# Sampled value rows fetched by SyncE at register addresses, two batches per transfer, with SyncE's queue in written order

## The chip, the core and the metric

The kernel runs on one core of one Trainium2 chip. A core has five engines with instruction queues of their own: TensorE (PE, with its weight loads shown as PEld), VectorE (DVE), ScalarE (ACT), GpSimd (POOL) and SyncE (SP), which here only issues DMAs. Sixteen DMA engines serve the core. The metric is the device time of one execution in microseconds (us), the median of the runs shown.

## What is computed

Block-sparse attention over 4 batches, 8 heads, 768 positions, head size 64, and then a mixture of experts with limited capacity on its output.

```python
block, n_blocks, window = 32, 24, 1
scores = scale * np.matmul(q, k.transpose(0, 1, 3, 2))
mask = np.abs(blk_i - blk_j) <= window
mask = mask | (blk_i == 0) | (blk_j == 0) | (blk_i == n_blocks - 1) | (blk_j == n_blocks - 1)
for qb in range(n_blocks):
    for kb in sampled_blocks[qb]:          # three per query block, the same for every batch and head
        mask[qb * block:(qb + 1) * block, kb * block:(kb + 1) * block] = True
...
attn = np.exp(scores); attn = attn / (np.sum(attn, axis=-1, keepdims=True) + 1e-09)
x = np.matmul(attn, v)                     # rows of all heads side by side: (3072, 512)
...
for e in range(8):                         # each row goes to its best expert, 80 rows at most for each
    h = np.maximum(x[tok_idx] @ w1[e], 0.0)
    out[tok_idx] = gate_w[tok_idx, None] * (h @ w2[e])
```

A query block sees at most eight key blocks: its window of three, the first and the last block, and the three that `sampled_blocks` names. Which blocks these are is known only when the kernel runs.

## The kernel before

The attention works in 24 groups. A group is one batch b and four neighbouring query blocks j (three at either end of the sequence); `ORDER` lists the pairs (j, b), batches 0 and 1 in its first half and 2 and 3 in its second, and `SWAP` exchanges the second and the third group of a half, so that groups 0 and 1 are both of batch 0. A group has two halves of four heads. A half goes through `products` (L352: scores of every block against its eight key blocks), `stage_a` (L360 on DVE: mask and minimum; L364 on ACT: exponent), `stage_b` (L372: transposes on PE; L338 or L340: copies out of PSUM, one on ACT and one on DVE) and `stage_c` (L386: the product with the values). On PE all of this stands in an order written by hand, in steps (`run_step`, `at`): four steps for a half, `products` at its step 0, `stage_b` at step 2, `stage_c` at step 5, which is one step after the `products` of the next half. The other engines' queues, SP's among them, are ordered by the compiler's scheduler.

Keys: `load_k` brings a batch's keys to the tile kt, and copies by DVE, ACT and POOL (`gather_k`, L291, L295, L245, L249) lay the key blocks of each group into one of two tiles kx. The sampled ones are read from kt at an address in a register; `load_blocks` (12 block numbers) and `load_own` (22 block numbers on each of DVE, ACT and POOL) put the numbers into registers (L261) at the very start. The first and the last block are copied by `fill_k_global` (L258, eight copies) whenever the batch of a kx tile changes.

Values: a group has for each of its query blocks a tile vw (the window's three blocks, 96 rows, and one global block) and a tile vd (three sampled blocks, 96 rows, and the other global block), in four sets (`SLOTS`). SP brings the windows (`load_qv`, L315) and, when the batch of a set changes, the global blocks (`load_v_global`, L238 to L242). The sampled rows are gathered by POOL: `gather_v` (L319), one indirect DMA for each query block and batch, 88 in all, with a table of row numbers, `idxV`, that DVE and POOL compute at the start (L172 to L181). For groups 1 to 5 (`VLATE`) these DMAs are put behind a key copy on POOL.

```python
nc.gpsimd.indirect_dma_start(
    out=vd[s][k][0:96, :], out_offset=None, in_=v[:, :],
    in_offset=bass.IndirectOffsetOnAxis(ap=idxV[0:96, b, qb:qb + 1], axis=0))
```

SP also loads the queries (L310, three tiles in turn), stores each group's rows to DRAM (`route1`, L409), writes zeros to the output (L754, behind the last query load) and loads rows for the blocks that see everything (`load_full`, L325 and L329). After the attention the experts run, from a store of the rows in DRAM and weights that SP loads (L869).

Of the kernel before, what the change touches and what calls it, by code (L numbers as in the profile page):

```python
# [24 lines left out]
P = 128  # L25
# [3 lines left out]
VW = HP * PW  # L29
# [6 lines left out]
VLATE = (1, 2, 3, 4, 5)  # L36
# [23 lines left out]
SWAP = (0, 1)  # L60
ORDER = []
for half in range(2):
    ORDER += [(j, 2 * half + i) for j in JO for i in range(2)]
# [5 lines left out]
SLOTS = [(0, 2, 1, 3, 0, 1, 2, 3, 0, 1, 2, 3)[n % NH] for n in range(len(ORDER))]  # L69
# [16 lines left out]
def kernel(  # L86
# [34 lines left out]
    nc.vector.tensor_copy(sf, si.rearrange("p (n t) -> p n t", t=2)[:, :, 0])  # L121
# [24 lines left out]
    with ExitStack() as actx:  # L146
# [23 lines left out]
        r32 = apool.tile([P, 1], F32, name="r32")  # L170
        for s in range(4):
            nc.gpsimd.iota(r32[32 * s:32 * s + 32, :], pattern=[[0, 1]], base=0, channel_multiplier=1,  # L172
                           allow_small_or_imprecise_dtypes=True)
        idxf = apool.tile([P, B, NBLK], F32, name="idxf")
        idxV = apool.tile([P, B, NBLK], U32, name="idxV")
        for s in range(NRAND):
            nc.vector.tensor_scalar(idxf[32 * s:32 * s + 32, 0, :], sbF[32 * s:32 * s + 32, :, s],
                                    float(BLK), r32[32 * s:32 * s + 32, :], op0=ALU.mult, op1=ALU.add)
        for b in range(1, B):
            nc.vector.tensor_scalar(idxf[0:96, b, :], idxf[0:96, 0, :], float(b * S), None, op0=ALU.add)  # L180
        nc.vector.tensor_copy(idxV[0:96], idxf[0:96])  # L181

# [34 lines left out]
        vw, vd = [[[(vp if s < 2 else apool).tile([P, VW], F32, name=f"{n}{s}{k}") for k in range(4)] for s in range(4)]  # L217
# [10 lines left out]
        def load_k(b):  # L228
            t = ktp.tile([P, HP, S], F32, name=f"kt{b % 2}", bufs=1)
            for c in ((slice(0, 2), slice(2, 4)) if b == 0 else (slice(0, 4),)):  # L230
                nc.sync.dma_start(t[:, c], kT[b][:, c])
            KT[b] = t

        def load_v_global(b, s):
            first, last = v[b * S:b * S + BLK, :], v[b * S + (NBLK - 1) * BLK:(b + 1) * S, :]
            for k in range(4):
                if k % 2 == 0:
                    nc.sync.dma_start(vw[s][k][0:32, :], last)  # L238
                    nc.sync.dma_start(vd[s][k][96:128, :], first)
                else:  # L240
                    nc.sync.dma_start(vw[s][k][96:128, :], first)
                    nc.sync.dma_start(vd[s][k][96:128, :], last)  # L242
# [61 lines left out]
        last_load = [None]  # L304

        def load_qv(b, j, s):

            t = qts[nq[0] % NQ]
            nq[0] += 1
            ld = nc.sync.dma_start(t, qn[b, j].rearrange("h d a c k -> (h d) a c k"))  # L310
            QT[b, j] = t
            last_load[0] = ld.ins
            for k, qb in enumerate(qbs_of(j)):
                lo = 32 if k % 2 == 0 else 0
                nc.sync.dma_start(vw[s][k][lo:lo + 96, :], v[b * S + (qb - 1) * BLK:b * S + (qb + 2) * BLK, :])  # L315

        def gather_v(b, j, s):
# [413 lines left out]
        if ORDER[1][1] == 1:  # L731
            load_k(1)
# [348 lines left out]
```

## Time and profile before

| | |
|---|---|
| median of 3 runs | 506.76 us (506.35 to 511.46) |
| the profiled execution | 510.95 us, its span 509.2 us |
| granted TensorE clock, mean over the span | 0.92 |
| PE busy | 407.6 us (80%) |
| DVE busy | 353.3 us (69%) |
| ACT busy | 310.4 us (61%) |
| POOL busy | 223.5 us (44%) |
| DMA | 109.34 MB, mean 215 GB/s |

A page of the profile and a packed trace of one execution are there. "Busy" is the time in which an engine worked on something; the time between is idle, and a view of the trace names what ended it: another engine's instruction, a DMA's landing, or "issue", when the engine waited for nothing that the profile shows. PEclk is the clock that TensorE was granted, as a share of 2.4 GHz; it is either 1.0 or 0.5 (1.2 GHz) at any time, and values between are means over a stretch. The DMA share is the mean busy share of the sixteen DMA engines; overlapping packets can take it a little over 1. Instructions that load registers are not counted as busy.

### The profile page before, as it was taken

Reading aid. Unit: us, or ns where it says so; the run is one execution under the profiler, and the core shown is the slowest. Engines: PE = TensorE matmul, PEld = TensorE weight load, DVE = VectorE, ACT = ScalarE, POOL = GpSimd, SP = SyncE. Lnnn points to the kernel's source line nnn. Section 1 sums busy time; section 2 is a strip of 40 time slices with the busy share of each in tenths; the row PEclk is TensorE's granted clock in tenths of the full one; section 3 lists DMA queues with packets and bytes.
Section 4 is the critical chain, followed back from the end, with each engine's and each line's share of the span. In section 5 each row is a group of like instructions: output and inputs, shape, how many; then the busy total and the mean of one; then the engine's idle time right before and its main releaser. Section 6 shows DMA issues by size and latency. Waiting matters only on the chain. (4 is left out here: it accounts for less than half of the span.)

```text
span 509.2 us, 16785 instructions
## 1 busy us (share of the span) xinstructions
PE 407.6 (80%) x6285; PEld 269.7 (53%) x6286; DVE 353.3 (69%) x1413; ACT 310.4 (61%) x748; POOL 223.5 (44%) x457
## 2 busy tenths in 40 slices
PE   0478877988898887778788899888758799898983
PEld 0245444665566554555556566665544565565651
DVE  3444665575668576887778879876986799787760
ACT  3244555565657776666656675788784475668740
POOL 3544854423542344554552435217436445242271
PEclk9888897898999988998999999997868899899997
DMA  8966889967664988896774877398406886889801
GB/s 250 285 178 191 226 257 261 260 191 239 172 177 145 302 239 223 216 270 201 224 217 116 253 210 202 111 311 289 125 23 192 283 273 209 291 295 310 324 17 30
DMA packets 57658, 109.34 MB, mean 215 GB/s; under 512 B 7196, under 2 KB 19485, under 8 KB 57187
## 3 DMA queue, kind: packets, MB, share of 16 engines
q1 hardware_dynamic: 50914, 88.17, 56.0%
q0 software_dynamic: 6656, 20.02, 14.8%
q8 instruction: 52, 0.85, 0.7%
q14 instruction: 36, 0.29, 0.2%
HBM read 94.38 MB, written 13.99 MB: 213 GB/s over the span
## 5 line engine op out<-in xcount | busy, mean ns | idle before, releaser
L319 POOL DMA_INDIRECT vd<-in_v_dram,idxV x88 | 84.6, 962 | 91.3 <-PE xb L386 71.4
L364 ACT ACTIVATE sb<-sb,mn 128x256 f32<-128x256 f32 (+1 forms) x192 | 86.5, 501 | 46.7 <-DVE mn L360 43.8
L360 DVE CUSTOM_DVE_ANT_1 sb<-S,quad 128x256 f32<-128x256 f32 (+1 forms) x192 | 74.9, 417 | 40.8 <-PE S L352 20.8
L372 PE MATMUL pt<-ident,sb 128*128 128x128 f32 (+1 forms) x384 | 72.5, 303 | 31.2 <-ACT sb L364 22.6
L352 PE MATMUL S<-kx,qt 64*32 64x256 f32 x1408 | 68.5, 437 | 15.4 <-DVE quad L207 11.7
L879 DVE TENSOR_TENSOR whl<-raw,whl 128x1024 fp32r<-128x1024 f32 x53 | 71.3, 1376 | 12.3 <-ACT whl L878 12.2
L878 ACT CAST whl<-raw 128x1024 fp32r<-128x1024 f32 x64 | 63.8, 1044 | 21.1 <-DMA raw<-in_w_dram 17.6
L372 PEld LDWEIGHTS pt<-ident,sb 128*128 128x128 f32 (+1 forms) x384 | 44.0, 152 | 53.6 <-ACT sb L364 33.9
L386 PE MATMUL xb<-vd,pts 128*32 128x65 f32 x1408 | 60.1, 230 | 10.2 <-issue 10.0
L386 PE MATMUL xb<-vw,pts 128*32 128x65 f32 x1408 | 59.0, 234 | 7.8 <-issue 6.8
L386 PEld LDWEIGHTS xb<-vd,pts 128*32 128x32 f32 x1408 | 42.9, 116 | 14.8 <-issue 14.8
L352 PEld LDWEIGHTS S<-kx,qt 64*32 64x32 f32 x1408 | 32.2, 142 | 34.3 <-issue 29.0
L386 PEld LDWEIGHTS xb<-vw,pts 128*32 128x32 f32 x1408 | 39.6, 115 | 18.2 <-issue 13.1
L879 POOL TENSOR_TENSOR whl<-raw,whl 128x1024 fp32r<-128x1024 f32 x11 | 29.7, 2707 | 42.3 <-ACT whl L878 42.3
L340 DVE COPY pts<-pt 128x512 f32<-128x512 f32 (+1 forms) x48 | 30.9, 643 | 23.0 <-PE pt L372 21.1
L926 PE MATMUL ph<-whl,xh 128*80 128x512 f32 x128 | 42.2, 401 | 0.9 <-ACT xh L886 0.6
L959 PE MATMUL po<-whl,hh 128*80 128x512 f32 x112 | 37.2, 403 | 2.4 <-DVE ob L965 2.0
L295 ACT COPY kx<-kt 128x128 f32 (+1 forms) x96 | 24.0, 296 | 20.4 <-PE S L352 12.3
L245 POOL COPY kx<-kt 128x128 f32 x84 | 22.4, 305 | 26.6 <-PE S L352 15.2
L525 DVE TENSOR_SCALAR_CACHE_REDUCE dump<-keyrow,keycol,cnt 128x640 bf16<-128x640 f32 (+5 forms) x36 | 32.4, 900 | 0.1
L585 ACT COPY xs<-xb 128x260 f32<-128x260 f32 (+2 forms) x64 | 23.3, 365 | 6.8 <-PE xb L386 6.0
L338 ACT COPY pts<-pt 128x512 f32<-128x512 f32 (+1 forms) x48 | 26.3, 548 | 1.5 <-PE pt L372 0.8
(210 smaller groups left out, 769.1 us busy)
## 6 DMA issues: line engine op xcount, KB each, us to landing
raw<-in_w_dram SPq DMA_DIRECT2D x64, 512.0 KB
vw<-in_v_dram SPq DMA_DIRECT2D x88, 195.0 KB
x_dram<-xs SPq DMA_DIRECT2D x24, 260.0 KB
vf<-in_v_dram SPq DMA_DIRECT2D x24, 260.0 KB
qt<-in_qn_dram SPq DMA_DIRECT2D x24, 256.0 KB
out_dram<-zero SPq DMA_DIRECT2D x12, 512.0 KB
kt<-in_kT_dram SPq DMA_DIRECT2D x3, 1536.0 KB
vw<-in_v_dram SPq DMA_DIRECT2D x32, 65.0 KB
```

What stands on the lines that cost most here:

```text
L319: nc.gpsimd.indirect_dma_start(out=vd[s][k][0:96, :], out_offset=None, in_=v[:, :], in_offset=bass.IndirectOffsetOnAxis(ap=idxV[0:96, b, q ...
L340: nc.vector.tensor_copy(dst, src)
L352: nc.tensor.matmul(banks[h][BLK * k:BLK * k + BLK, i].rearrange("p (g a) c -> p g (a c)", g=2), lhsT=QT[b, j][d, hp, :, k], rhs=keys, star ...
L360: ins = nc.vector.tensor_tensor_reduce(out=sb, in0=st, in1=quad[0:r, j, :, None].to_broadcast([r, 8, 32]), scale=-0.125, scalar=3.0e38, op ...
L364: order["s"] = nc.scalar.activation(p, p, AF.Exp, bias=mn, scale=-1.0).ins
L372: nc.tensor.transpose(pt[:, (2 * i + c) * r:(2 * i + c + 1) * r], p[:, c * P:(c + 1) * P], ident[0:r, 0:r])
L386: nc.tensor.matmul(xb[place:place + 32, o:o + 65], lhsT=pts[:, c * r + BLK * k:c * r + BLK * k + BLK], rhs=(vw, vd)[c][s][k][:, hd * 65:hd ...
L525: cmp = nc.vector.tensor_scalar(d, keyrow[:, lo * P:hi * P], key, c, op0=ALU.is_le, op1=ALU.add, accum_out=c)
L878: nc.scalar.copy(hi, t)
L879: eng.tensor_sub(lo, t, hi.bitcast(F32))
L926: nc.tensor.matmul(ps[0:SLOT, :], lhsT=l[:, cs], rhs=r[:, ws], start=(i == 0), stop=(i == 3 * HP - 1))
L959: nc.tensor.matmul(po[0:SLOT, :], lhsT=l[:, cs], rhs=r[:, ws], start=(i == 0), stop=(i == 23))
```

## The change

- The indirect DMAs of POOL and the table `idxV` are gone. The sampled rows come by SP's DMAs, one for each query block and sampled block, whose source row stands in a register of SP. `load_rows` loads the 12 (or 9) block numbers of a pair of groups into SP's registers.
- A transfer covers two batches: groups 2p and 2p+1 are the same query blocks j in two batches (`SWAP` is gone), and vw and vd are now two sets, one for each pair in turn, with room for four query blocks and two batches. A window's DMA brings 192 rows, a sampled block's 64. For the first pair alone the batches are loaded apart.
- SP's DMAs of the attention stand in the order in which they are written. At step 2 of each even group come the values of the next pair; the store of zeros has a step of its own.
- `load_own` (22 register loads on each of three engines) moves behind the first scores (DVE) and exponents (ACT).
- With `SWAP` gone, a kx tile changes its batch less often: of the nine calls of `fill_k_global` for a whole tile (groups 1 to 4 and 12 to 16), the six for groups 2, 3, 4, 14, 15 and 16 fall away: 48 copies, 36 of them on DVE.
- The copy of the numbers to `sf` moves from DVE to ACT, and a POOL drain late in the attention is dropped.

```diff
-VLATE = (1, 2, 3, 4, 5)
-    if half in SWAP:
-        ORDER[12 * half + 1], ORDER[12 * half + 2] = ORDER[12 * half + 2], ORDER[12 * half + 1]
+ORDER = [(j, 2 * half + i) for half in range(2) for j in JO for i in range(2)]
...
-    nc.vector.tensor_copy(sf, si.rearrange("p (n t) -> p n t", t=2)[:, :, 0])
+    nc.scalar.copy(sf, si.rearrange("p (n t) -> p n t", t=2)[:, :, 0])
...
-        idxV = apool.tile([P, B, NBLK], U32, name="idxV")
...
-        vw, vd = [[[(vp if s < 2 else apool).tile([P, VW], F32, name=f"{n}{s}{k}") for k in range(4)] for s in range(4)]
+        vw, vd = [[(vp if i < 1 else apool).tile([P, 4, 2, VW], F32, name=f"{n}{i}") for i in range(2)]
...
+        def load_v_global(i, b):
+            first, last = vrows[0:BLK, b], vrows[(NBLK - 1) * BLK:, b]
+            for dst, lo, k0, src in ((vw[i], 0, 0, last), (vw[i], 96, 1, first), (vd[i], 96, 0, first),
+                                     (vd[i], 96, 1, last)):
+                nc.sync.dma_start(dst[lo:lo + 32, k0:4:2, b % 2], src[:, None].to_broadcast([BLK, 2, VW]))
...
-            for r, e in enumerate((ENG.DVE, ENG.Activation, ENG.Pool)):
-                vals = read_blocks(slice(NRAND + r, (NBLK - 1) * NRAND, NRAND), [e])
+            for r, (e, last) in enumerate(((ENG.DVE, "v"), (ENG.Activation, "s"), (ENG.Pool, None))):
+                with tc.issue_after(order[last]) if last else nullcontext():
+                    vals = read_blocks(slice(NRAND + r, (NBLK - 1) * NRAND, NRAND), [e])
...
+        def load_rows(pair):
+            if 2 * pair < len(ORDER):
+                qbs = qbs_of(ORDER[2 * pair][0])
+                c = min(qbs) * NRAND
+                vals = read_blocks(slice(c, c + len(qbs) * NRAND), [ENG.SP])
+                for k, qb in enumerate(qbs):
+                    for r in range(NRAND):
+                        ROWS[pair, k, r] = vals[(qb - min(qbs)) * NRAND + r] * BLK
...
+        def load_v(pair, bs=None):
...
+            def window(k):
+                lo, row = 32 if k % 2 == 0 else 0, (qbs[k] - 1) * BLK
+                nc.sync.dma_start(vw[i][lo:lo + 96, k, at_b], vrows[row:row + 96, bs])
+            def sampled(k, r):
+                nc.sync.dma_start(vd[i][32 * r:32 * r + 32, k, at_b], vrows[bass.ds(ROWS[pair, k, r], BLK), bs])
...
-        with tc.manual_schedule(engines={ENG.PE}):
+        with tc.manual_schedule(engines={ENG.PE, ENG.SP}):
+            run(load_k(0))
+            load_q(0)
+            load_v_global(0, 0)
+            load_rows(0)
+            fs, ks = load_v(0, slice(0, 1)), load_k(1)
+            run(fs[:10] + ks[:1] + fs[10:] + ks[1:])
+            load_q(1)
+            nc.sync.dma_start(wg, w_gate.rearrange("(c p) e -> p c e", p=P))
+            load_v_global(0, 1)
+            run(load_v(0, slice(1, 2)))
+            load_rows(1)
             for n, (j, b) in enumerate(ORDER):
+                if n == 0:
+                    prefetch(0)
+                    at(1, load_own)
                 at(0, lambda n=n: prefetch(n + 1))
-                at(2 if (n + 2) % NH in (1, 5) else 0, lambda n=n: loads(n + 2))
+                at(0, lambda n=n: load_q(n + 2))
...
+                if n and n % 2 == 0 and n + 2 < len(ORDER):
+                    def next_v(pair=n // 2 + 1):
+                        if pair in (6, 7):
+                            for b in range(2, 4):
+                                load_v_global(pair % 2, b)
+                        run(load_v(pair))
+                        load_rows(pair + 1)
+                    at(2, next_v)
```

## Rows read from the trace of the kernel before

**Rows 1.** The busy time of each engine in stretches of the span: before the first score product, from there to the first `products` of group 5, from there to the first of group 12, and from there to the end of the last `stage_c`. After each engine's busy time the number of its instructions; the last three columns are the mean granted clock, the DMA share and the DMA rate.

```profile
0.00:14.96 14.96, 0.70 (x2) 0.53 (x3) 6.68 (x46) 5.52 (x25) 6.06 (x28) 1.00 0.84 257
14.96:105.78 90.82, 71.04 (x1194) 43.67 (x1194) 49.49 (x270) 42.85 (x117) 46.53 (x93) 0.87 0.86 237
105.78:200.33 94.55, 79.76 (x1527) 54.35 (x1524) 62.41 (x312) 63.92 (x173) 40.00 (x107) 0.94 0.73 211
200.33:367.90 167.57, 141.22 (x2971) 96.39 (x2967) 131.81 (x621) 113.20 (x304) 74.26 (x190) 0.95 0.72 211
```

**Rows 2.** The timeline from the start to the first copies out of PSUM: DVE, ACT and the first score products of PE. Columns: start, duration, engine, line, operation, in brackets the idle time before.

```profile
3.75 0.15 DVE L168 COPY capv<-misc 128x1 f32<-128x1 f32 x1
8.79 0.75 DVE L177 TENSOR_SCALAR idxf<-sbF,r 32x24 f32<-32x24 f32 x3 [4.89 <-POOL tri L141]
...
9.57 0.23 DVE L189 TENSOR_TENSOR dif<-sbF,qbI 128x72 f32<-128x72 f32 x1
...
14.21 0.18 DVE L207 COPY quad<-m 32x32 f32<-32x32 f32 x1
14.42 3.23 DVE L249 COPY kx<-kt 128x64 f32<-128x64 f32 x20
22.42 0.42 DVE L360 CUSTOM_DVE_ANT_1 sb<-S,quad 128x256 f32<-128x256 f32 x1 [4.77 <-remote]
...
22.89 1.71 ACT L364 ACTIVATE sb<-sb,mn 128x256 f32<-128x256 f32 x4 [9.22 <-DVE mn L360]
24.67 0.59 ACT L338 COPY pts<-pt 128x512 f32<-128x512 f32 x1
...
14.96 3.37 PE L352 MATMUL S<-kx,qt 64*32 64x256 f32 x32 [11.74 <-DVE quad L207]
```

**Rows 3.** The register loads of L261, by engine: duration in ns (least, median, most), and the first and the last start in us. Each engine's shorter one loads 12 numbers, its longer one 22.

```profile
L261 ACTq TENSOR_LOAD <-sbi x2: 986/2814/4643, 2.4 to 3.4; - x2
L261 DVEq TENSOR_LOAD <-sbi x2: 1120/3041/4962, 2.4 to 3.7; - x2
```

**Rows 4.** All engines between 2 and 8 us, columns as in the first group: the loads of the first keys and queries.

```profile
2.00:8.00 6.00, 0.70 (x2) 0.50 (x2) 0.59 (x4) 0.00 (x0) 1.00 (x7) 1.00 0.98 341
```

**Rows 5.** The timeline of POOL's indirect DMAs (before the first score of DVE, and around the `stage_c` that begins at 33.00) and of PE in that `stage_c`.

```profile
17.85 0.92 POOL L319 DMA_INDIRECT vd<-in_v_dram,idxV  x1 [0.30 <-issue]
...
33.34 0.92 POOL L319 DMA_INDIRECT vd<-in_v_dram,idxV  x1 [0.30 <-issue]
...
34.91 0.29 PE L386 MATMUL xb<-vw,pts 128*32 128x65 f32 x3 [0.43 <-issue]
36.38 0.22 PE L386 MATMUL xb<-vw,pts 128*32 128x65 f32 x1 [1.18 <-issue]
```

**Rows 6.** PE's matmuls and weight loads of L386 alone, in the windows that hold one `stage_c` each, for the fifteen near which POOL issued indirect DMAs: the first and the sum of the five up to 90 us, and the first and the sum of the ten after that. The second column is the window's length, then PE and PEld busy, clock, DMA share and rate.

```profile
33.00:38.42 5.42, 2.37 (x64) 1.55 (x64) 1.00 0.57 150
...
sum 15.42, PE 9.31 PEld 6.46; mean PE 1.86 PEld 1.29
...
120.85:126.02 5.17, 3.06 (x64) 1.95 (x64) 0.81 0.93 273
...
sum 32.20, PE 20.40 PEld 13.89; mean PE 2.04 PEld 1.39
```

**Rows 7.** The same for ten others, with no indirect DMA near: one in full DMA traffic, and the sum of the ten.

```profile
189.08:190.22 1.14, 1.11 (x48) 0.95 (x48) 1.00 0.97 296
...
sum 11.41, PE 11.20 PEld 9.56; mean PE 1.12 PEld 0.96
```

**Rows 8.** PE on either side of a quiet `stage_c`: its last matmuls, and the first transposes of the half that comes next.

```profile
226.74 0.30 PE L386 MATMUL xb<-vd,pts 128*32 128x65 f32 x8
228.40 0.33 PE L372 MATMUL pt<-ident,sb 128*128 128x128 f32 x1 [1.36 <-ACT sb L364]
```

**Rows 9.** All engines in the stretches at half clock that begin during or right after the `stage_c` and score product named in the groups above: the first and the sum of the four up to 94 us, and the sum of the four between 124 and 234 us.

```profile
21.61:28.43 6.82, 4.89 (x84) 3.30 (x88) 2.93 (x14) 2.60 (x6) 0.00 (x0) 0.50 1.05 317
...
sum 17.07, PE 14.76 PEld 8.74 DVE 5.58 ACT 6.83 POOL 3.65; mean PE 3.69 PEld 2.18 DVE 1.40 ACT 1.71 POOL 0.91
...
sum 13.64, PE 13.35 PEld 8.86 DVE 5.93 ACT 7.24 POOL 4.46; mean PE 3.34 PEld 2.22 DVE 1.48 ACT 1.81 POOL 1.12
```

**Rows 10.** Groups of instructions by line: copies of the global key blocks (one group for each engine) and POOL's indirect DMAs; count, busy us, mean ns, idle before.

```profile
L258 DVE COPY kx<-kt 128x128 f32<-128x128 f32 x54 | 9.1, 228 | 6.3 <-PE misc L491 3.9 <-PE cs L540 2.1 <-PE S L352 0.3
L258 ACT COPY kx<-kt 128x128 f32<-128x128 f32 (+1 forms) x26 | 6.2, 282 | 7.0 <-PE cs L540 3.5 <-PE misc L491 3.5
L319 POOL DMA_INDIRECT vd<-in_v_dram,idxV x88 | 84.6, 962 | 91.3 <-PE xb L386 71.4 <-issue 13.5 <-DVE tmp L193 2.3
```

**Rows 11.** SP's timeline (the time from one issue to the next lies in the start column): a global block of 32 rows, four windows of 96 rows, and the last issue before and the first after a long pause. The last two rows are of the DMA view: the size of a window's transfer, and the packets, MB and share of POOL's queue.

```profile
10.65 0.31 SPq L241 DMA_DIRECT2D vw<-in_v_dram  x1
...
12.25 1.84 SPq L315 DMA_DIRECT2D vw<-in_v_dram  x4
...
21.84 0.34 SPq L310 DMA_DIRECT2D qt<-in_qn_dram  x1
38.84 0.33 SPq L409 DMA_DIRECT2D x_dram<-xs  x1
...
vw<-in_v_dram SPq DMA_DIRECT2D x88, 195.0 KB
...
q0 software_dynamic: 6656, 20.02, 14.8%
```

More of the change, by code (lines that the diff above doesn't have):

```diff
@@ L302, in gather_k, with load_q @@
             return todo
-        last_load = [None]
-        def load_qv(b, j, s):
+        def load_q(n):
+            if n >= len(ORDER):
+                return
+            j, b = ORDER[n]
             t = qts[nq[0] % NQ]
             nq[0] += 1
-            ld = nc.sync.dma_start(t, qn[b, j].rearrange("h d a c k -> (h d) a c k"))
+            nc.sync.dma_start(t, qn[b, j].rearrange("h d a c k -> (h d) a c k"))
             QT[b, j] = t
[L312 to L317, printed above, removed]
-            for k, qb in enumerate(qbs_of(j)):
-                nc.gpsimd.indirect_dma_start(
-                    out=vd[s][k][0:96, :], out_offset=None, in_=v[:, :],
-                    in_offset=bass.IndirectOffsetOnAxis(ap=idxV[0:96, b, qb:qb + 1], axis=0))
+        ROWS = {}
+        def load_rows(pair):
[7 more added lines that the diff above has]
+        def load_v(pair, bs=None):
+            j, b = ORDER[2 * pair]
+            i, qbs = pair % 2, qbs_of(j)
+            bs = bs or slice(b, b + 2)
+            at_b = slice(bs.start % 2, bs.start % 2 + bs.stop - bs.start)
+            def window(k):
[3 more added lines that the diff above has]
+                nc.sync.dma_start(vd[i][32 * r:32 * r + 32, k, at_b], vrows[bass.ds(ROWS[pair, k, r], BLK), bs])
+            return ([lambda k=k: window(k) for k in range(len(qbs))]
+                    + [lambda k=k, r=r: sampled(k, r) for k in range(len(qbs)) for r in range(NRAND)])
         def load_full(b):
@@ L376, in stage_b, with stage_c @@
             return [pts[:, 2 * i * r:2 * (i + 1) * r] for i in range(len(ps))]
-        def stage_c(xb, j, s, items):
+        def stage_c(xb, j, s, xb_b, items):
             r = rows_of(j)
@@ L578, in f @@
                     def f():
-                        stage_c(xb, j, s, [(store[i], 4 * half + i) for i in ids])
+                        stage_c(xb, j, n // 2 % 2, b % 2, [(store[i], 4 * half + i) for i in ids])
                     return f
@@ L679, in fresh @@
             return n < bufs or ORDER[n - bufs][1] != ORDER[n][1]
-        def fresh_v(n):
-            before = [m for m in range(n) if SLOTS[m] == SLOTS[n]]
-            return not before or ORDER[before[-1]][1] != ORDER[n][1]
         def prefetch(n):
@@ L711, in prefetch @@
                     at(GLATE + i * (8 - GLATE) // len(todo), g)
-                    if n in VLATE and i == len(todo) - 1:
-                        def h():
-                            with tc.issue_after(order["p"]):
-                                gather_v(b, j, SLOTS[n])
-                        at(7, h)
                 else:
                     at(i * 6 // len(todo), f)
-        def loads(n):
-            if n < len(ORDER):
-                j, b = ORDER[n]
-                load_qv(b, j, SLOTS[n])
-                if n not in VLATE:
-                    gather_v(b, j, SLOTS[n])
-                if fresh_v(n):
-                    load_v_global(b, SLOTS[n])
@@ L739, with second @@
             for n, (j, b) in enumerate(ORDER):
                 m = n % NH
+                if n == 0:
+                    prefetch(0)
+                    at(1, load_own)
                 at(0, lambda n=n: prefetch(n + 1))
-                at(2 if (n + 2) % NH in (1, 5) else 0, lambda n=n: loads(n + 2))
+                at(0, lambda n=n: load_q(n + 2))
+                if n == 0:
+                    def second():
+                        for b in range(2):
+                            load_v_global(1, b)
+                        run(load_v(1))
+                        load_rows(2)
+                    at(0, second)
```

63 lines of the change are left out of this document (14 added, 49 removed).

## The prediction

> **What bounds the kernel now.** I read the stretches of the span first [rows 1]. The last `stage_c` ends at 367.9 us; the experts take the remaining 141 us, and the change does not touch their work, so everything is decided before. From the first score on PE is busy 78 to 84% of each stretch, DVE 54 to 79%, the DMA engines 72 to 86%; POOL is busy half of the time or less. So PE's own queue sets the pace. Until 14.96 us PE has almost nothing to do. Then I asked what PE loses inside its work, by looking at one kind of work that is the same 48 times, `stage_c`. Ten of them take 1.14 us each, as the sum 11.41 shows [rows 7]. Fifteen others take 47.62 us together, 3.2 us each, for the same matmuls [rows 6]. In the long ones PE stands still for 0.4 to 1.2 us at a time in front of instructions with no wait ("issue"), and all fifteen lie beside POOL's indirect DMAs, which follow each other every 1.2 us [rows 5]. Traffic as such is not it: a quiet one ran with the DMA engines 97% busy, a long one with 57% [rows 6, 7]. The same shows at the first scores: the products end on PE at 18.33, yet DVE gets them at 22.42, and in between POOL issues gathers [rows 2, 5]. PE's clock follows: eight stretches at half clock begin in or just behind such places [rows 9].
>
> **Gathers leave POOL.** 88 instructions of 0.96 us go [rows 10]; POOL is idle half of the time, so its 84.6 us count as 0 (up to 1 if a key copy was late). What counts is PE. Excess of the long `stage_c`: 47.62 - 15 x 1.14 = 30.5 us. The window from 120.85 had a mean clock of 0.81, some 1 us of half clock; I leave 29.4. Not all comes back. After a quiet `stage_c` PE waited 1.36 us for ACT before its next transposes [rows 8], a wait that a long one swallows; the ten later long ones average 3.22 us, 2.08 over 1.14, so 0.72 of 2.08 would be left, 35%. That is the low end, 10.3 us; the high end is all, 29.4. In the first stretches DVE is far from full (54%), later it is at 79%, so I take 60%: 17.6 us. The Trainium skill ("SBUF — State Buffer", Who interferes with whom) says the opposite: PE and ACT never wait on anyone. The 1.14 against 3.2 us disagrees in time, though not yet in cause; by the page this term would be 0.
>
> **Half clock.** In the eight stretches PE was busy 14.76 + 13.35 = 28.1 us [rows 9]; at full clock half of it, 14 us, is saved. Other idle time can still lower the clock, and DVE paces some of these halves: I take 7, between 0 and 14.
>
> **Register loads behind the first scores.** Now DVE is done with `capv` at 3.90, loads 22 numbers for 4.96 us [rows 2, 3], starts on the mask at 8.79 with three instructions for the table, and runs from 9.57 to 14.39 to `quad`; 20 key copies end at 17.65, the products 0.7 us later. After the change the same chain of 4.8 us starts at 3.9: mask 8.7, copies 12.0, products 12.7. The keys (2 x 768 KB) and queries (256 KB) are there: 2.05 MB had come by 8.0 us [rows 4]. With the 4.1 us of waiting gone as well, DVE's first score comes at 12.8, 9.6 us sooner. But the loads now stand between the exponents and the copies out of PSUM: exponents end 2.2 us after the first score, at 15.0, ACT's 4.64 us [rows 3] make it 19.6, where the first copy stood at 24.67 [rows 2]. Behind them wait these copies, and behind those PE's `stage_c`. Gain 5; it is 9.6 if the loads find cover, and 1 if the scores still wait 4.1 us.
>
> **The key copies.** 48 of 80 global copies go: 36 x 0.228 us on DVE, 12 x 0.28 on ACT, 11.6 us [rows 10], most of it beside PE's work. In the last stretch DVE is nearly as full as PE: I take 2, between 0 and 5.
>
> **SP.** It gains 144 DMAs for sampled rows and twelve register loads, and loses 40 window DMAs and half of the 64 global ones. A 32-row DMA takes SP 0.31 us, a 96-row one 0.46 [rows 11]; one with 64 rows and a register is not in the trace. Bounds: 0.31, and the 1.22 us from one gather to the next on POOL [rows 5]; I take 0.45, since the queue and the kind of issue are those of the first. A pair then costs 12 x 0.45 + 4 x 0.7 + 1.1 for the register loads, about 9 us (at 1.22: 19 us), against the 29 us that a pair lasts now (353 us for twelve [rows 1]): 0 on the path. Queued behind SP's waits are the loads of the pair after, and for those PE's `stage_c`. The written order also ends pauses such as the one from 22.2 to 38.84, where SP stood before a store of rows with the loads of two groups behind it [rows 11]. But the loads themselves set a floor. Up to 105.78 us the DMA engines were busy 0.84 x 14.96 + 0.86 x 90.82 = 90.7 us [rows 1]: no more than 15 us can be won there, and my terms put 5 + 0.6 x 9.7 + 0.5 x 7.4 = 14.5 us there. Rates that close to 100% don't last, and the second batch's keys are now needed one group sooner: -3, between 0 and -8.
>
> **Sum.** 5 + 17.6 + 7 + 2 - 3 = 28.6 us. The profiled execution took 510.95 us, 1.4 of it outside its span, so its like would take 482.4. It is 4.2 us above the median; I take the saving off the median: 506.76 - 28.6 = 478.2. Low ends together give 1 + 10.3 + 0 + 0 - 8 = 3.3 us (503), high ends 9.6 + 29.4 + 14 + 5 = 58 us (449).
>
> **Rivals.**
> 1. *DMA becomes the bound.* The stalls go, but two sets of values instead of four leave little slack: a pair's loads may start only when the pair before the last is done with its set. For it: DMA shares of 0.86 before 105.78 and 0.72 later at 10% less time leave bursts near 1. Against: those bursts exist now, and nothing on PE waited for values. It keeps some 10 to 18 us of the 28.6: 489 to 497.
> 2. *The stalls stay,* since they come with the gathered rows' arrival and not with POOL's issuing; the rows now arrive by SP. For: in the traffic of the long ones the gathers' packets are always there too. Against: windows of 195 KB with rows of the same length come all the time, and quiet `stage_c` run under 97%. Left are 1 us of the start and 2 of copies: 503. The page named above, which lets PE wait on nobody, would lead to this result.
> 3. *Slower: the sampled rows are slow in SP's queue.* One mechanism: 64 rows a DMA, each behind SP's waits, at a rate well below that of the gathers (20 MB in 14.8% of the span [rows 11], 266 GB/s). A pair moves 1.6 MB of sampled rows and about 4.3 MB of the rest; at the 296 GB/s of a full stretch [rows 7] the rest takes 15 us. If the sampled rows come below 100 GB/s, a pair needs 31 us instead of 29 and PE waits in every pair: 506.8 + 11 x 2 - 5 for the start = 524. At POOL's 1.22 us each, 133 KB would come at 109 GB/s, just above that point.
> 4. *Nothing changes*, because the scheduler's new order on DVE and ACT costs what PE wins: 507.
>
> **How the numbers follow.** Forecast (462 to 489) 0.60; DMA bound (489 to 500) 0.18; stalls stay (503) 0.08; slower 0.10; nothing 0.04. A measurement of this kernel can tell about 1%, 5 us, from no change. Faster: 0.60 + 0.18 and 0.02 of the third, 0.80; same 0.10; slower 0.10. The range leaves out the slower and the unchanged case and the far low end: 458 to 503.
>
> **What would show it.** All `stage_c` at 1.1 to 1.3 us; DVE's first score within 0.3 us of the end of the products, near 13 us; a gap of 5 us on DVE and ACT right after it; PE's clock in 14.96 to 105.78 above 0.87, and fewer half-clock stretches; the last `stage_c` near 340; POOL busy some 85 us less; the experts' part still near 141 us. I am wrong if long `stage_c` remain with no gathers on POOL (2), if PE waits on landings of vw or vd (1, 3), or if the first copy out of PSUM comes later than 21 us.

## The result, and the profile after

On the chip of the first measurement the changed kernel took 492.25 us (median of 4 runs, 488.19 to 497.25) and the kernel before 507.64 (506.35 to 511.46): ratio 0.966, 95% interval 0.957 to 0.975. The forecast was 478. The profiled execution took 488.19 us with a span of 486.4.

That ratio does not hold on every chip. All runs of one comparison share a chip, and later comparisons fell on others (the number of the first chip is not on record; it may be chip 0 too). Some runs came 1.5 to 3% above the fastest of their kernel and are left out of the ratios; without them the median of the kernel before on chip 10 is 472.4 us, and that of the kernel with key copies made again (below) 499.65.

| chip | kernel before, us | changed kernel, us | ratio, 95% interval |
|---|---|---|---|
| first measurement | 507.64 | 492.25 | 0.966 (0.957 to 0.975) |
| 0 | 509.31 | 491.18 | 0.965 (0.956 to 0.973) |
| 10 | 473.62 | 491.39 | 1.039 (1.033 to 1.046) |
| 4 | 475.43 | only variants of it, 489 to 502, and one at 548 | |
| 2 | 474.98 | only variants of it, 494 and 500 | |

The changed kernel takes the same time in all three comparisons, 491 to 492 us; it is the kernel before that has two times. So the result is faster by 3.5% twice and slower by 3.9% once, where all seven runs of the kernel before (471 to 485 us) lie below all four of the changed one (489 to 495), and the explanation has to hold both. Chips where the kernel before takes 507 to 509 us are called the first kind below, those where it takes 474 to 475 us the second. Each numbered chip was used in one comparison only, so whether the kind goes with the chip or with the hour is not told apart.

First the stretches of the changed kernel (columns as in [rows 1]): up to the first score product, to the first `products` of group 5, to the first of group 12, to the end of the last `stage_c`.

```profile
0.00:8.98 8.98, 0.70 (x2) 0.52 (x3) 5.62 (x38) 4.74 (x21) 2.09 (x20) 1.00 0.75 250
8.98:98.79 89.81, 68.48 (x1193) 46.00 (x1193) 45.63 (x246) 45.27 (x125) 13.10 (x60) 0.89 0.92 232
98.79:180.55 81.76, 71.84 (x1527) 49.98 (x1524) 60.96 (x306) 60.41 (x162) 19.11 (x82) 0.98 0.72 191
180.55:345.64 165.09, 139.84 (x2971) 96.19 (x2967) 129.49 (x606) 111.50 (x298) 43.47 (x162) 0.94 0.81 222
```

The first products begin 6.0 us sooner, DVE's first score 11.0 (11.46 against 22.42 us [rows 2]), group 5 begins 7.0 us sooner, group 12 19.8, and the last `stage_c` ends 22.3 us sooner. The second stretch is as long as before (89.81 against 90.82 us): what the start won was not added to there, although the stalls of [rows 6] are gone: 27 of the 48 `stage_c` take 1.11 or 1.12 us. What PE does in it instead shows in the waits, up to the end of the last `stage_c` (us in total, times, longest; the 5.9 us are the start, before the first product), and in group 2's first `stage_c`: its window (length, PE and PEld busy, clock, DMA share, rate) and PE's timeline.

```profile
PE xb L382 <- DMA vd<-in_v_dram: 9.1, 9, 1.9
PE S L348 <- DVE kx L225: 5.9, 1, 5.9
PE xb L382 <- DMA vw<-in_v_dram: 5.1, 3, 2.4
PE xb L382 <- issue: 2.1, 2, 1.3
```

```profile
45.09:58.21 13.12, 4.24 (x64) 2.62 (x64) 0.63 1.05 241
```

```profile
46.73 0.30 PE L382 MATMUL xb<-vw,pts 128*32 128x65 f32 x2 [1.33 <-DMA vw<-in_v_dram]
48.34 0.30 PE L382 MATMUL xb<-vw,pts 128*32 128x65 f32 x2 [1.31 <-DMA vw<-in_v_dram]
51.08 0.42 PE L382 MATMUL xb<-vw,pts 128*32 128x65 f32 x2 [2.44 <-DMA vw<-in_v_dram]
...
55.64 0.40 PE L382 MATMUL xb<-vd,pts 128*32 128x65 f32 x2 [1.17 <-DMA vd<-in_v_dram]
```

A `stage_c` that takes 1.1 us when its values are there runs from 45.09 to 58.20 us, matmul after matmul released by the landing of the next rows. In SP's timeline the same stretch looks like this (start, duration of the merged group):

```profile
25.38 7.94 SPq L314 DMA_DIRECT2D vd<-in_v_dram  x12
34.18 0.36 SPq L287 DMA_DIRECT2D qt<-in_qn_dram  x1
...
39.34 1.90 SPq L311 DMA_DIRECT2D vw<-in_v_dram  x4
41.44 11.96 SPq L314 DMA_DIRECT2D vd<-in_v_dram  x12
```

Twelve sampled DMAs of 32 rows take SP 7.94 us, 0.66 us each, and the first twelve of 64 rows 11.96 us, 1.0 us each; the forecast had 0.45 for the latter.

### The profile page after: what moved, and what is told of

The parts are those of the page before. It is cut to its first block, busy times and chain, and to the rows that moved or that the text cites. A ratio compares the mean times of both kernels' runs of the same rounds, so it can differ in the third digit from the quotient of the medians.

```text
span 486.4 us, 16932 instructions
## 1 busy us (share of the span) xinstructions
PE 395.4 (81%) x6286; PEld 267.9 (55%) x6286; DVE 344.4 (71%) x1369; ACT 308.3 (63%) x737; POOL 141.4 (29%) x365
## 5 line engine op out<-in xcount | busy, mean ns | idle before, releaser
L368 PE MATMUL pt<-ident,sb 128*128 128x128 f32 (+1 forms) x384 | 67.4, 294 | 21.6 <-ACT sb L360 20.6
L348 PE MATMUL S<-kx,qt 64*32 64x256 f32 x1408 | 67.0, 434 | 10.6 <-DVE kx L225 5.9
L877 DVE TENSOR_TENSOR whl<-raw,whl 128x1024 fp32r<-128x1024 f32 x53 | 67.0, 1294 | 8.7 <-ACT whl L876 8.3
L368 PEld LDWEIGHTS pt<-ident,sb 128*128 128x128 f32 (+1 forms) x384 | 42.6, 148 | 40.5 <-ACT sb L360 35.5
L382 PE MATMUL xb<-vd,pts 128*32 128x65 f32 x1408 | 57.2, 236 | 9.4 <-DMA vd<-in_v_dram 7.2
L382 PE MATMUL xb<-vw,pts 128*32 128x65 f32 x1408 | 56.8, 240 | 7.8 <-DMA vw<-in_v_dram 5.1
L469 POOL TENSOR_SCALAR tab<-oh_all 128x8 bf16<-128x8 f32 x23 | 5.3, 232 | 167.2 <-DVE oh_all L453 167.1
L382 PEld LDWEIGHTS xb<-vd,pts 128*32 128x32 f32 x1408 | 41.9, 121 | 11.7 <-issue 9.9
L924 PE MATMUL ph<-whl,xh 128*80 128x512 f32 x128 | 43.8, 415 | 0.6 <-ACT xh L884 0.6
L877 POOL TENSOR_TENSOR whl<-raw,whl 128x1024 fp32r<-128x1024 f32 x11 | 30.0, 2727 | 48.6 <-ACT whl L876 48.5
L957 PE MATMUL po<-whl,hh 128*80 128x512 f32 x112 | 36.2, 393 | 1.9 <-DVE ob L963 1.9
```

The source lines that it names most:

```text
L348: nc.tensor.matmul(banks[h][BLK * k:BLK * k + BLK, i].rearrange("p (g a) c -> p g (a c)", g=2), lhsT=QT[b, j][d, hp, :, k], rhs=keys, star ...
L368: nc.tensor.transpose(pt[:, (2 * i + c) * r:(2 * i + c + 1) * r], p[:, c * P:(c + 1) * P], ident[0:r, 0:r])
L382: nc.tensor.matmul(xb[place:place + 32, o:o + 65], lhsT=pts[:, c * r + BLK * k:c * r + BLK * k + BLK], rhs=(vw, vd)[c][s][:, k, xb_b, hd * ...
L877: eng.tensor_sub(lo, t, hi.bitcast(F32))
L924: nc.tensor.matmul(ps[0:SLOT, :], lhsT=l[:, cs], rhs=r[:, ws], start=(i == 0), stop=(i == 3 * HP - 1))
L957: nc.tensor.matmul(po[0:SLOT, :], lhsT=l[:, cs], rhs=r[:, ws], start=(i == 0), stop=(i == 23))
```

## The experiments

**Gathers on POOL again.** The twelve sampled DMAs of a pair became eight gathers (POOL's indirect DMAs); the table of indices came back with them, the POOL drain that the change had dropped did not.

```
...
-   nc.sync.dma_start(vd[i][32 * r:32 * r + 32, k, at_b], vrows[bass.ds(ROWS[pair, k, r], BLK), bs])
+   nc.gpsimd.indirect_dma_start(
+       out=vd[i][0:96, k, c % 2, :], out_offset=None, in_=v[:, :],
+       in_offset=bass.IndirectOffsetOnAxis(ap=idxV[0:96, c, qbs[k]:qbs[k] + 1], axis=0))
...
```

> The changed kernel with its sampled rows fetched by 88 indirect DMAs on POOL again (0.96 us each, one per query block and batch, 96 rows), into the same two-batch tiles and at the same steps; SP has no register loads and no sampled DMAs. The rest of the change stays. Theory (POOL's issuing stops PE): PE's idle pieces of over 0.35 us in front of instructions that wait for nothing, 3 us in sum in the attention part of the changed kernel against 15 in the kernel before, come back to 10 to 15 us, many stage_c are at 2 to 3.2 us instead of 1.12, and the time is 500 to 508 us. Rival (they came with the old order of loads or of key copies, not with POOL): stage_c stay at 1.12 us and the time is within 3 us of 492.

On chip 4, 501.76 us beside 475.43 of the kernel before. The time is in the range of the theory, its mechanism is not there, and 9 us of the time lie behind the last matmul (see the end of the next section). The windows of six `stage_c` with gathers within 2 us of them:

```profile
67.80:68.97 1.17, 1.17 (x64) 1.00 (x64) 1.00 1.09 292
...
sum 6.97, PE 6.95 PEld 6.00; mean PE 1.16 PEld 1.00
```

1.16 us each, with POOL's gathers beside them, against 3.2 in [rows 6]. These six are not all: 35 `stage_c` lie within 2 us of a gather, and 21 of them take at most 1.21 us, the longest 4.9. In front of their matmuls PE stands 8.9 us without a wait, in 7 pieces; the changed kernel, without gathers, has 8.1 us in 6 on chip 10. The kernel before at 475 us was the first sign that this chip differs from the first.

**Gathers of nearly no bytes.** In the changed kernel, 88 gathers of 32 bytes a row go to a tile that nobody reads.

```
...
+   nc.gpsimd.indirect_dma_start(
+       out=spare[0:96, nsp[0], :], out_offset=None, in_=v.rearrange("t (a e) -> (t a) e", e=8),
+       in_offset=bass.IndirectOffsetOnAxis(ap=idxV[0:96, c, qbs[k]:qbs[k] + 1], axis=0))
...
```

> The changed kernel with its SP DMAs as they are, and beside them 88 more indirect DMAs on POOL of 96 rows of 32 bytes into a spare tile that nobody reads (3 KB instead of 200 KB each; a table of indices as in the kernel before is worked out for them). Theory (the issuing, not the data): the idle pieces of PE in front of instructions that wait for nothing return, 10 us or more in sum, long stage_c beside the indirect DMAs, 499 to 508 us. Rival (the arrival of 200 KB of gathered rows makes the stalls): with 1.5% of the bytes nothing of it, stage_c at 1.12 us, 492 within 3 us plus at most 1 us for the table.

On the same chip, 548.43 us, slower than either theory, for a reason of its own: with nothing to wait for, POOL issued all 88 in one row, and its key copies stood behind them. Two rows of PE:

```profile
62.74 2.61 PE L371 MATMUL S<-kx,qt 64*32 64x256 f32 x32 [40.57 <-POOL kx L237]
...
121.89 2.62 PE L371 MATMUL S<-kx,qt 64*32 64x256 f32 x32 [25.81 <-POOL kx L237]
```

The total says nothing on the question, but five `stage_c` between 65 and 94 us, with gathers going on all the time, do:

```profile
65.28:66.51 1.23, 1.23 (x64) 1.06 (x64) 0.89 0.10 16
...
sum 5.84, PE 5.83 PEld 5.01; mean PE 1.17 PEld 1.00
```

A sixth there, at 86.84 us, takes 1.96, busy throughout, at a clock of 0.50. On chip 4 neither the issuing nor the arrival of gathers brings the short stalls of [rows 5].

**The second pair loaded batch by batch.**

```
                         for b in range(2):
                             load_v_global(1, b)
-                        run(load_v(1))
+                            run(load_v(1, slice(b, b + 1)))
```

> The changed kernel, but the values of the second pair of groups (groups 2 and 3) are loaded batch by batch, as those of the first pair are: first all rows of batch 0 (four global DMAs, four windows, twelve sampled), then all of batch 1, in DMAs of half the size. Theory (in the changed kernel group 2 stands for rows of batch 1, which only group 3 needs; DMA engines full from 36 us on): group 2's first stage_c, which ends at 58.20 us, ends 7 to 9 us earlier, the 13.7 us stretch at half clock at 48.6 us shrinks, and the time falls by 4 to 9 us to 483 to 488. Rival (bytes up to the third pair are the floor, so PE only waits one group later): products of group 4 start where they do now and the time is 492 within 3 us. Second rival (SP's issuing, 0.51 us per sampled DMA, is the limit): group 2 comes 3 us earlier or less, and group 3 later.

On chip 4, 489.08 us (ratio to the kernel before 1.035, interval 1.025 to 1.046). The interval holds the changed kernel's 1.039 on chip 10, so no gain is shown, as the first rival said. Group 2's `stage_c` ends at 50.70 as the theory said, but PE then waits for something else, whose load SP had behind the second batch:

```profile
61.35 2.44 PE L348 MATMUL S<-kx,qt 64*32 64x256 f32 x32 [7.32 <-DMA qt<-in_qn_dram]
```

**Register loads in front of the scores again.**

```
...
                 vals = load_blocks(j)
+                load_own()
...
-                    at(1, load_own)
```

> The changed kernel with the register loads of DVE, ACT and POOL in front of the first scores again, the rest as changed. Theory (the start's gain is lost in the wait for values in groups 1 and 2): the first copy out of PSUM comes 4 to 7 us later than 17.70 us, group 2's first stage_c ends at 58 us as before, and the time is within 3 us of 492. Rival (the prediction's term): 5 us slower, 497.

On chip 4, 494.69 us, ratio 1.044 (1.034 to 1.054). It overlaps with the changed kernel's 1.039 on chip 10, so these two do not tell 3 us from 0. The first score came at 16.25 us, not 11.46, but the first copy out of PSUM only 0.80 us later than in the changed kernel, 18.50 against 17.70, not the 4 to 7 expected by either theory; group 2's first `stage_c` ends at 56.77 us. The row of the changed kernel shows why the copies gain so little:

```profile
17.70 0.58 ACT L334 COPY pts<-pt 128x512 f32<-128x512 f32 x1 [4.07 <-issue]
```

The 4.66 us of ACT's register load now lie in front of that copy.

**The kernel before once more.** The same kernel, profiled on chip 0.

> The kernel before, unchanged, profiled beside the next three, because in the comparison with the first four experiments it took 475.43 us where it had taken 507.64. Theory (there the stalls of PE beside POOL's indirect DMAs are missing, and the rest is as it was): about 475 us again if this is the same chip, PE's idle pieces over 0.35 us in front of instructions without a wait at 5 us or less in sum instead of 15, stage_c beside the indirect DMAs at 1.14 us, DVE's first score soon after the first products. Rival (that chip is faster throughout): every operation and every transfer is some 6% shorter, stalls included. If it takes 507 us, the chips differ from call to call.

507.9 us: this chip has the stalls of the first profile, so neither the theory nor its rival could show here. Its rows stand beside those of another chip below.

**The changed kernel once more.** On chip 0, beside the one above.

> The changed kernel, unchanged, against the kernel before on the same chip as the last one. Theory (the gain of the change is the end of stalls that not every chip has): where the kernel before takes 475 us, this one takes 485 to 495, so it is slower there by 2 to 4%, with the wait for values in groups 1 and 2 as in the first profile. Rival (that chip is faster throughout): 460 us, ratio 0.966 as first measured.

491.18 us beside 509.31: the first ratio again. Group 2's first `stage_c` ends at 56.69 us.

**Late register loads alone.** In the kernel before, `load_own` moved behind the first scores as in the change.

> The kernel before with one part of the change alone: DVE, ACT and POOL load their registers of sampled blocks behind the first scores. Prediction's term: 5 us faster than the kernel before (0 to 9.6). Theory (a start that is sooner meets the arrival of values in the next groups): first copy out of PSUM 5 to 7 us sooner, but the time within 3 us of the kernel before.

On chip 0, 509.28 us, ratio 0.998 (0.993 to 1.003). The first copy out of PSUM came at 21.33 us, against 22.20 in the kernel before on that chip: 0.9 sooner, not 5 to 7, and at the end there is no gain that an interval of 0.5% either way lets one see.

**Global key copies made again.**

```
-            if fresh(n, 2):
+            if fresh(n, 2) or n % 12 in (2, 3, 6, 7, 10, 11):
```

> The changed kernel with the copies of the global key blocks into both key tiles made again in 12 more groups (96 small copies more, 72 on DVE at 0.23 us and 24 on ACT at 0.28 us), the blocks being the same ones. The change had taken out 48 of them, worth 2 us by the prediction (0 to 5). Prediction's term: 4 us slower than the changed kernel (0 to 10). Rival (hidden beside PE's work and the waits for values): within 2 us.

On chip 0, 499.65 us (501.44 over all four runs) beside 491.18: the 96 copies cost 8.5 us (5.9 us at the last `stage_c` of the two profiles). The intervals of the two ratios to the kernel before, 0.973 to 0.996 and 0.956 to 0.973, just meet. If half as many cost half as much, the 48 copies that the change took out are worth 3 to 4 us.

**Gathers on POOL again, on another chip.** The first experiment's kernel.

> The changed kernel with its sampled rows by 88 indirect DMAs on POOL, the same kernel as in the first of these experiments, on whatever chip comes. There the stage_c beside the indirect DMAs took 1.11 to 1.35 us, no stall, and the kernel before ran in 475 us. Theory 1 (whether POOL's indirect DMAs stop PE differs from chip to chip): if the kernel before takes 505 to 512 us here, stage_c beside the indirect DMAs take 2 to 4 us in this kernel too, with PE's idle pieces of 0.4 to 0.5 us each, and it takes 505 to 520 us, more than the 502 of the other chip; if the kernel before takes about 475 us, this one takes 502 again without those stalls. Theory 2 (the layout of the value tiles or the order of the loads makes the stalls): beside a kernel before at 507 us this one still has none, and takes 502 us.

It came to chip 2, a chip of the second kind: 500.21 us beside 474.98. Of the 34 `stage_c` within 2 us of a gather 21 take at most 1.21 us, and the two longest (3.69 and 5.50 us) wait in part for landings. This kernel has no run on a chip of the first kind, so for the stalls there issuing and arrival are not told apart.

**Pair by batch, with the queries between.**

```
...
+                if n == 1:
+                    def third():
+                        load_v_global(1, 1)
+                        run(load_v(1, slice(1, 2)))
+                        load_rows(2)
+                    at(0, third)
...
```

> The changed kernel with the values of groups 2 and 3 loaded batch by batch, and group 3's queries, 256 KB, issued by SP between the two batches and not behind both. In the split without that, group 2's first stage_c ended at 50.70 us and not at 58.20, but PE then stood 7.32 us for those queries, from 54 to 61.35. Theory: that wait goes, products of group 3 start near 54 us, and the time is 5 to 9 us below that of the changed kernel: 0.947 to 0.955 of the kernel before on a chip where the changed kernel is at 0.965. Rival (the bytes up to the third pair are the floor): PE waits for values of group 3 or 4 in its place, products of group 4 start where they do in the changed kernel, ratio 0.96 to 0.97.

On chip 2, 494.24 us, ratio 1.034 (1.023 to 1.046): not the version that beats both. The wait for the queries is gone and group 3's products begin sooner, but group 4 now stands for its rows:

```profile
74.66 0.27 PE L382 MATMUL xb<-vd,pts 128*32 128x65 f32 x2 [2.11 <-DMA vd<-in_v_dram]
76.30 0.40 PE L382 MATMUL xb<-vd,pts 128*32 128x65 f32 x2 [1.37 <-DMA vd<-in_v_dram]
```

Its first `stage_c` lasts from 71.58 to 80.44 us, and in the changed kernel it ends at 81.39. So the rival holds in that PE now stands for group 4's values, and not in that group 4's products start where they did: they start at 65.41 us, 7.7 sooner, and the gain goes in the wait behind them. Nor is the number of bytes the floor, as the first 80 us of this kernel and of the kernel before on the same chip show:

```profile
0.00:80.00 80.00, 49.86 (x1011) 33.65 (x1012) 42.01 (x238) 42.66 (x128) 13.47 (x71) 0.91 0.85 219
```

```profile
0.00:80.00 80.00, 54.34 (x1113) 34.51 (x1114) 51.75 (x295) 45.05 (x136) 46.70 (x112) 0.98 0.97 271
```

The DMA engines have room (0.85), and the kernel before moved more. From 27.6 to 75.4 us SP issues one DMA after another almost without a pause, the 32-row ones every 0.6 to 0.7 us.

**The kernel before on a chip of the second kind.**

> The kernel before, unchanged, for its profile beside the first of these two on the same chip. Theory 1: stage_c beside the indirect DMAs 2 to 4 us if the time is 505 to 512 us, 1.1 to 1.4 us if it is 470 to 478 us. Theory 2: they are long at either time.

On chip 2, 476.27 us. Here is the same program on the two chips. First PE's idle time in front of `stage_c`'s matmuls without a wait, on chip 0 and then on chip 2 (total, times, longest):

```profile
PE xb L386 <- issue: 16.6, 37, 1.1
```

```profile
PE xb L386 <- issue: 10.9, 7, 3.5
```

Then the windows of the same six `stage_c` (groups 2, 6, 7, 13, 15 and 16, first halves, all beside gathers), chip 0 and chip 2:

```profile
120.03:124.47 4.44, 2.21 (x64) 1.45 (x64) 1.00 0.93 295
...
sum 22.26, PE 13.12 PEld 9.12; mean PE 2.19 PEld 1.52
```

```profile
101.69:102.82 1.13, 1.12 (x64) 0.96 (x64) 1.00 0.95 269
...
sum 8.02, PE 7.64 PEld 6.52; mean PE 1.27 PEld 1.09
```

3.7 us each against 1.3, at the same DMA share, beside the same gathers (their median is 924 ns on both). These six are among the longest on chip 0; all 48 `stage_c` together take 89.1 us there and 71.2 on chip 2. The many short idle pieces are gone on chip 2; seven longer ones stay. DVE's first score follows the products at once there, 18.15 after 18.13 us, where [rows 2] have 22.42 after 18.33 and chip 0 has 19.34 after 18.27. The last `stage_c` ends at 330.08 us on chip 2 and 366.75 on chip 0. Theory 1 is right in that the stalls were there in some comparisons, each on its chip, and not in others; why, no run here shows.

**The changed kernel on a third chip.**

> The changed kernel, unchanged, once more beside the kernel before, on whatever chip comes. On two chips the kernel before has taken 475 us and shown no stall of PE beside POOL's indirect DMAs, on two others 507 to 509 us with them; four kernels made from the changed one took 489 to 502 us on the first two. Theory (the gain is the end of those stalls and nothing else outweighs its losses): if the kernel before takes about 475 us here, the changed one takes 488 to 496, ratio 1.03 to 1.04, with the same waits for arriving values as in its first profile; if the kernel before takes 507 us, ratio 0.96 to 0.97. Rival (the chips where the kernel before is quick are quicker in all): ratio 0.96 to 0.97 on either, 460 us beside 475.

On chip 10, 491.39 us beside 473.62, ratio 1.039: the theory, and not a chip that is quick in all.

## Why the prediction was right, and where it was not

The sign and the range held on the chip of the measurement, but 492.25 us lies outside the 462 to 489 that had 0.60, and the sum is partly luck: the stalls were worth more than forecast, the loads cost far more, and the two errors offset each other in part. PE's time up to the end of the last `stage_c`, us (idle pieces over 0.15 us):

| | before, first chip | changed, first chip | before, chip 2 | changed, chip 10 | gathers back, chip 2 |
|---|---|---|---|---|---|
| busy | 292.7 | 280.9 | 270.1 | 277.5 | 279.0 |
| idle without a wait | 22.7 | 3.4 | 12.1 | 13.0 | 16.6 |
| waits for other engines | 50.8 | 45.7 | 45.4 | 46.0 | 48.6 |
| waits for landings | 0.0 | 14.2 | 0.9 | 13.2 | 4.7 |
| end of the last `stage_c` | 367.9 | 345.6 | 330.1 | 351.1 | 350.4 |
| mean granted clock | 0.93 | 0.94 | 0.97 | 0.94 | 0.94 |

*Gathers leave POOL, with half clock (17.6 and 7 us): the mechanism fits chips of the first kind, the size was too small.* On the first chip idle time without a wait falls by 19.3 us and PE's busy time, which half clock stretches, and so do matmuls that stand apart (64 take 2.37 us at a clock of 1.00 in [rows 6]), by 11.9: 31 us where 24.6 were forecast (30 us between the profiles of chip 0). The kernel before itself takes 509.31 us with stalls and 474.98 without: 34 us. So the cut to 60% and the halving of the clock's term were together too careful. On chips without the stalls this term is nothing. No run puts the gathers back on a chip of the first kind, so that they, and not the old order of loads, bring the stalls there is argued from where the stalls lie. The Trainium skill ("SBUF — State Buffer", Who interferes with whom) says that PE never waits on anyone; chip 2 agrees (1.12 us in group 2's first, beside gathers), chip 0 does not (3.87 us in the same one), though no run shows what PE waits for there. The forecast took one trace's stalls for the kernel's; they were that chip's as well.

*Register loads behind the first scores (5 us): failed.* "Gain 5", read from the first copy, stood 7.0 us sooner on the first chip, 17.70 against 24.67 us; but the two kernels that move the loads alone show 0.8 and 0.9 us at that copy, and at the end nothing clear of noise. The scores gain 5 us and the loads, now in front of the copy, take it back; the forecast had counted the copy's old place with that profile's 4.1 us of stall in it.

*Key copies (2 us, 0 to 5): in the range, the size small,* 3 to 4 us by the kernel that adds them, if cost goes with number.

*SP (0) and the floor of the loads (-3): this is the step that failed.* On the first chip PE waits 14.2 us for landings of `vd` and `vw`, all in the first three groups, where the kernel before waited for none; the forecast had 3, at most 8. Without stalls to remove, the change costs 491.39 - 472.4 = 19 us. The table splits the 21 us up to the last `stage_c` (chip 10 less chip 2): 12.3 us more waits for landings, 7.4 us more busy time at a lower clock, 1.5 us of the rest. In the wait shown above the mean clock is 0.63. Two places hold most of it. In the changed kernel on chip 10, group 2's first `stage_c` ends at 57.07 us, in the kernel before on chip 2 at 46.56: 10.5 us. Between the first `products` of groups 12 and 13, where the second half's other batch comes in, the one takes 13.95 us (181.68 to 195.63), the other 9.30 (171.43 to 180.73): 4.7 us, of which PE stands 2.9 for a key copy of DVE. SP issued that batch's keys at 181.43 us, behind twelve sampled DMAs that took it 12.95 us; in the kernel before on chip 2 at 156.12. The rest is spread over the groups after that, and its cause stays open. The loads of the first part, by the mean busy share of the DMA engines and the rate (last two columns), for the kernel before on chip 2, the changed kernel on chip 10, and the changed kernel with gathers on chip 2:

```profile
29.00:38.00 9.00, 8.47 (x161) 5.34 (x161) 5.25 (x28) 6.15 (x18) 5.43 (x11) 1.00 0.87 246
...
0.00:58.00 58.00, 37.53 (x792) 23.48 (x793) 35.38 (x202) 30.28 (x93) 32.94 (x82) 0.97 0.94 264
```

```profile
29.00:38.00 9.00, 5.88 (x116) 4.51 (x100) 2.97 (x16) 4.42 (x12) 0.99 (x4) 0.81 0.58 153
...
0.00:58.00 58.00, 33.14 (x573) 22.43 (x574) 25.71 (x148) 26.02 (x80) 7.99 (x45) 0.85 0.91 234
```

```profile
29.00:38.00 9.00, 7.11 (x142) 4.92 (x142) 4.42 (x22) 3.90 (x10) 5.12 (x13) 0.81 1.04 265
...
0.00:58.00 58.00, 33.13 (x574) 22.59 (x574) 26.63 (x155) 24.93 (x77) 30.86 (x73) 0.91 1.01 263
```

Two things are in these rows. First, SP alone does not keep the DMA engines busy while it issues DMAs of 32 rows of one batch: 0.58 and 153 GB/s from 29 to 38 us, and up to 58 us 234 GB/s x 58 us = 13.6 MB against 15.3 MB. The forecast asked whether a pair's issues fit into a pair's time, which they do, and not whether they fit where the engines have to be full. Second, this is not all. With gathers back on POOL's queue the engines are full (265 GB/s), and PE's waits for landings fall from 13.2 to 4.7 us, so most of them come with the sampled rows in SP's queue. Yet group 4's first `stage_c` still ends at 81.60 us, as late as in the changed kernel (81.39), 10.9 us later than in the kernel before on chip 2 (70.67). Other waits have taken the place of the landings; the two longest:

```profile
29.43 2.62 PE L364 MATMUL S<-kx,qt 64*32 64x256 f32 x32 [2.82 <-POOL kx L235]
...
51.27 1.44 PE L384 MATMUL pt<-ident,sb 128*128 128x128 f32 x6 [4.98 <-issue]
```

The first is a key copy that stood behind sixteen gathers in POOL's queue, the second has no wait. What of the 4.7 us comes from the order of the groups (batch 1 follows at once, so its keys, global rows and windows are needed one group sooner) and what from two batches in one transfer is open: no kernel here puts back either alone. The second counts for something: with the second pair by batch, group 2's first `stage_c` ended at 50.70 us (chip 4) and not at 57.07.

*The rivals.* The first, "DMA becomes the bound", at 489 to 497 us, is what came, with the sign of being wrong that the prediction had named for it: PE waits on landings of `vd` (9.1 us) and `vw` (5.1 us). It had 0.18; the traffic of the early stretch, 0.86 of the engines' time in [rows 1], should have given it more. Its slack of two sets was not the limit: the waits are in the first pairs, for which both sets are free. The second, stalls that stay, is wrong on the first chip; the fourth, nothing, is wrong everywhere. The third, slower, is the result on chip 10, where there is no stall to remove, though not by its mechanism of PE waiting in every pair.

*The signs.* First score at the end of the products (11.46 us; forecast 13), first copy at 17.70 (19.6), POOL 141.4 us instead of 223.5 (82 less; 85), experts 140.8 us (141): right. Last `stage_c` at 345.64 (340) and the early clock (0.89, above 0.87): the one missed by the landings, the other just met.

One difference remains, the 9 us between the kernel with gathers back (500.21 and 501.76 us) and the changed kernel (491.39). Its last `stage_c` ends within 2 us of that of the changed kernel on chip 10 (350.35 and 352.56 against 351.10). The 9 us come at the very end: from the last indirect DMA to the end of the span it has 16.6 us, the changed kernel 7.7. POOL's drains (duration in ns: least, median, most; first and last start in us), of the gathers' kernel on chip 2, the changed kernel on chip 10 and, late in the attention, the kernel before on chip 2:

```profile
L1087 POOLq DRAIN  x3: 46/98/8570, 489.2 to 498.4; - x3
```

```profile
L1075 POOLq DRAIN  x3: 46/108/1383, 490.7 to 492.7; - x3
```

```profile
L611 POOLq DRAIN  x1: 8142/8142/8142, 299.6 to 299.6; - x1
```

The kernel before pays 8.1 us for its drain in the attention and 1.4 at the end; the kernels with gathers back, without that drain, pay 8.6 at the end (a semaphore instruction of POOL, 2.3 us instead of 0.5, makes up the rest). So these 9 us are not the price of gathers beside PE; no run puts the drain back.

## What to carry to other kernels

A stall with no wait in the trace may belong to the chip it was recorded on: before a change is built to remove it, time the kernel on a second chip, and ask what the change is worth where there is no stall. When loads are moved from one queue to another or asked for sooner, sum the bytes that must have landed by each of the first groups and compare with the rate of a full stretch; a floor of the loads is read there, not from an average over a pair. A gain at the start counts only as far as the next landing that PE has to wait for. When a variant takes back one part of a change, look where its time lies before reading its total: 9 us of the gathers' kernel were behind the last matmul.

## What the runs showed of the hardware

The same program took 473.6 to 475.4 us on three chips and 507.6 and 509.3 in two other comparisons, with PE idle in front of instructions that wait for nothing, some 0.45 us at a time, 16.6 us in 37 pieces on chip 0, beside gathers whose own durations (924 ns) are the same as on chip 2. Chip 2 has seven longer pieces instead, 10.9 us. A drain on POOL took 8.1 us after 88 gathers and 8.6 at the end of a program that had not drained before, 1.4 us in one that does without these gathers. All kinds of chip show a rarer, longer gap; here is one of the changed kernel on chip 0, in the middle of a `stage_c`, with the DMA engines above 100% busy by the profile's count:

```profile
225.37 0.32 PE L382 MATMUL xb<-vd,pts 128*32 128x65 f32 x8 [4.32 <-issue]
```

A single packet of the instruction queue q8 lies between 222 and 223 us, in that gap. In the fourteen traces there are nineteen idle pieces of PE over 2.4 us without a wait up to the last `stage_c`; sixteen have a packet of that queue in them or up to 0.5 us before, where by chance some seven would. That PE waits for its code there fits, but no experiment tried it.
